# Laying out the weight loads of a DMA-bound decode kernel for the DMA engines

## The chip, the cores and the metric

The kernel runs on one core of one Trainium2 chip. The metric is the device time of one execution in microseconds (us). Most executions of one kernel agree within 0.1%, and all within 0.25%: the kernel before took between 2662.8 and 2669.3 us over all runs of this study, and its median was between 2663.6 and 2664.8 in every group of runs made together. So a difference of about 1 us between medians of two groups says little.

## The reference, cut to what matters

A decode step with batch 2 and one token goes twice through the same two blocks: attention over a long cache, and a small MLP.

```python
B, Sq, D = 2, 1, 576
H, Sk, Dh = 32, 16384, 128             # k_cache, v_cache: (B, H, Sk, Dh) in bf16, 268 MB each
q = (x @ wq) ...                       # wq (576, 4096)
p = softmax(q @ k_cache^T * Dh**-0.5);  o = p @ v_cache
x = x + o @ wo                         # wo (4096, 576)
...                                    # B block: hs = shift(gelu(LN(x) @ w1)) @ w2  (w2 576x576)
h2 = gelu(LN(x1) @ w3) @ w4            # w3 (576, 4608), w4 (4608, 576)
# x = x + A(x); x = x + B(x); x = x + A(x); x = x + B(x)
```

With one token the shifted input of `w2` is zero; the kernel still loads `w2` and multiplies it with zeros. All of K and V is read once per layer, which is over 1.06 GB in 508 loads of 2 MB (one of the 64 head-batch units is kept from the first layer to the second). The weights are some 40 MB of 1106 MB. 576 is 4 times 128 plus 64, so `wq` and `w3` have a last tile of only 64 rows.

## The kernel before

All loads go through one queue (the SP engine's) into a ring of 12 slots. A load is issued as soon as the readers of the slot that it overwrites are done.

```python
def kv(src, u, h):            # a half of K or V of a unit: 128 partitions x 16 KB
    ap = src[b, hh].rearrange("(t p j) d -> t p (j d)", t=2, p=128)[h]
    return lambda e, v: e.dma_start(v, ap)

def krows(w, k, c0, c1):      # wq, w3, w2: tile k, one row per partition
    if k < self.KT - 1:
        ap = w[k * 128:(k + 1) * 128, c0:c1]
        return lambda e, v: e.dma_start(v, ap)
    ap = w[k * 128:D, c0:c1]                                # the last 64 rows
    return lambda e, v: e.dma_start(v[self.p0:128, :], ap)  # p0 = 64: partitions 64 to 127

def jrows(w, j0, n):          # wo, w4: n blocks of 128 rows, rows of 1,152 bytes
    ap = w[j0 * 128:(j0 + n) * 128, :].rearrange("(j p) n -> p j n", p=128)
    return lambda e, v: e.dma_start(v.rearrange("p (j n) -> p j n", j=n), ap)

# the order of the loads of a layer (cut)
for i, u in enumerate(order):
    K(u, 0), K(u, 1)
    if l == 0 and i == 0: w2 in 5 loads (krows)
    if i >= 1: V(order[i - 1], 0), V(order[i - 1], 1)   # before every 16th: wo of 8 heads (jrows)
w3 in 5 loads (krows), w4 in 3 loads of 12 blocks (jrows); after layer 0: wq in 5 loads
```

Every 16 units `group_out` divides 16 columns by their sums, multiplies them with 8 heads of `wo` and adds to `x`. ... (cut: scores, half on PE and half on DVE; exponentials on ACT; the sum over V on PE.)

## Time and profile before

| what | number | where it is read |
|---|---|---|
| median time | 2663.6 us (3 runs), 2664.0 (4 runs with the changed kernel) | timings |
| DMA traffic | 1110.9 MB, mean 417 GB/s | page, DMA part |
| busy share | DVE 74%, PE 59%, ACT 41%, DMA about 99% | page, parts 1 and 3 |
| undisturbed slices | 425 to 427 GB/s | page, part 2 |

The rate of the 40 equal slices of the execution (66.6 us each), and the DMA queues (packets, MB, share of the time of 16 engines), from the page of the kernel before:

```profile
GB/s 393 426 426 427 424 419 426 426 426 408 426 426 426 426 407 426 426 426 425 357 401 421 426 426 422 426 427 425 426 392 426 426 427 426 407 426 426 427 426 300
q1 hardware_dynamic: 94072, 1106.16, 99.0%
q8 instruction: 270, 4.42, 0.7%
```

The kernel is bound by DMA: 1110.9 MB at 427 GB/s take 2602 us of 2663. The other 60 us are the dips: some at about 407 (a `wo` load is in that slice), the layer change (357, 401), and the end (392, 300). Queue q8 is the fetching of instructions.

What the `wo` load does to the queue, from the timeline of the SP engine (start, us until the next entry, what). It issues `wo` at 616.42, and then the next load of V takes 36 us to issue, and the one after it goes out at 657.1:

```profile
616.42 4.25 SPq L307 DMA_DIRECT2D ring<-in_A_wo_dram  x1
620.71 38.36 SPq L296 DMA_DIRECT2D ring<-in_A_v_cache_dram  x2
659.11 0.93 SPq L296 DMA_DIRECT2D ring<-in_A_k_cache_dram  x2
```

Waiting for the ring is not the reason: by the kernel's own semaphore counts the readers of these two slots were done at 613.5 and 623.3 us. So it was the queue that held the load up, behind `wo`.

The DMA issues of `wo` (count, KB each, us from issue to landing), and the layer change in the view by stretches (stretch in us; length; busy time and instructions of PE, PEld, DVE, ACT, POOL; clock; DMA share; GB/s):

```profile
ring<-in_A_wo_dram SPq DMA_DIRECT2D x8, 1152.0 KB, 48.7
1309.00:1361.00 52.00, 26.08 (x679) 24.69 (x680) 8.36 (x34) 4.71 (x12) 0.00 (x0) 0.50 1.02 334
```

Note the DMA share of 1.02 beside 334 GB/s: over these 52 us (w3, w4 and wq) the engines were occupied all the time, but moved a fifth less than they can. The loss is slow packets, not waiting. Around the two 64-row tiles of this stretch, one packet in twenty of `wq` took over 848 ns and of `w3` over 1,089 ns, where the median over the whole execution is 309 and 347.

The end, from the timeline: after the last piece of w4 lands, 60 matmuls, and then the output:

```profile
2658.41 1.76 PE L457 MATMUL misc<-gt,ring 128*128 128x2 bf16 x60 [2.75 <-DMA ring<-in_B_w_dram]
2661.87 0.28 SPq L405 DMA_DIRECT2D out_dram<-prod  x1
```

**Two groups of engines.** The trace also holds a record of every completion. A load over 128 partitions runs on 16 DMA engines and leaves 16 records. Sorted by time they fall into eight early and eight late ones. The records around the second `wo` load of the kernel before (us):

```
                 early eight        late eight
K unit 32, h 1   650.3 .. 652.5     659.6 .. 662.0
wo heads 8-15    653.1 .. 655.4     662.5 .. 664.9
V unit 31, h 0   663.3 .. 664.0     667.4 .. 669.8
V unit 31, h 1   668.2 .. 668.9     672.3 .. 674.7
```

The early eight are some 9 us ahead (I call this the lead). Behind the `wo` load they run dry, and lose about 5 us of it. The late eight go on: 2.9 us for `wo`, then 4.9 for the next load. Elsewhere a K or V load takes the early eight 4.89 us and the late eight 4.99 us on average: an interval of the late eight is 4.89 without an instruction fetch in it and about 5.08 with one, averaged over the eight. Of 497 such intervals 254 were of the long kind, and 263 fetches fell into the same stretch of time.

### The profile page before, as it was taken

Reading aid. Unit: us, or ns where it says so; the run is one execution under the profiler, and the core shown is the slowest. Engines: PE = TensorE matmul, PEld = TensorE weight load, DVE = VectorE, ACT = ScalarE, POOL = GpSimd, SP = SyncE. Lnnn points to the kernel's source line nnn. Section 1 sums busy time; section 2 is a strip of 40 time slices with the busy share of each in tenths; the row PEclk is TensorE's granted clock in tenths of the full one; section 3 lists DMA queues with packets and bytes.
Section 4 is the critical chain, followed back from the end, with each engine's and each line's share of the span. In section 5 each row is a group of like instructions: output and inputs, shape, how many; then the busy total and the mean of one; then the engine's idle time right before and its main releaser. Section 6 shows DMA issues by size and latency. Waiting matters only on the chain.

```text
span 2663.4 us, 74240 instructions
## 1 busy us (share of the span) xinstructions
PE 1558.8 (59%) x34587; PEld 1461.0 (55%) x34587; DVE 1979.6 (74%) x2649; ACT 1098.5 (41%) x1681; POOL 0.8 (0%) x10
## 2 busy tenths in 40 slices
PE   4665565555556555556467565665556556556654
PEld 4555555555555555555457555555555555555554
DVE  5877877777777777787559777777777777777773
ACT  3444344344334434434235344344334434434431
POOL 0000000000000000000000000000000000000000
PEclk8666666666666666666566666666666666666665
DMA  9999999999999999999999999999999999999998
GB/s 393 426 426 427 424 419 426 426 426 408 426 426 426 426 407 426 426 426 425 357 401 421 426 426 422 426 427 425 426 392 426 426 427 426 407 426 426 427 426 300
DMA packets 94380, 1110.90 MB, mean 417 GB/s; under 512 B 8756, under 2 KB 26744, under 8 KB 26744
## 3 DMA queue, kind: packets, MB, share of 16 engines
q1 hardware_dynamic: 94072, 1106.16, 99.0%
q8 instruction: 270, 4.42, 0.7%
q14 instruction: 38, 0.31, 0.0%
HBM read 1106.13 MB, written 0.00 MB: 415 GB/s over the span
## 4 chain that ended last, share of the span: by engine, by line
DMA 67%; PE 11%; DVE 8%; another core or an unknown queue 8%; ACT 4%; SPq 1%; issue 1%
DMA ring<-in_A_v_cache_dram 35%; DMA ring<-in_A_k_cache_dram 28%; DVE sd L572 5%; PE ops L617 5%; PE tps L539 4%; DMA ring<-in_B_w_dram 4%; ACT ktsb L543 3%; DVE prod L569 3%; PE sps L557 1%; PE misc L590 1%; DMA ring<-in_A_wq_dram 1%; ACT p L603 1%; SPq L301 0%; PE misc L457 0%
## 5 line engine op out<-in xcount | busy, mean ns | idle before, releaser
L572 DVE TENSOR_REDUCE sd<-prod 128x8 f32<-128x1024 bf16 x1024 | 1249.0, 1220 | 35.4
L543 ACT ACTIVATE ktsb<-tps 128x1024 bf16<-128x1024 bf16 x1024 | 992.7, 1028 | 514.6 <-PE tps L539 509.1
L539 PE MATMUL tps<-ident,ring 128*128 128x128 bf16 x8192 | 829.2, 268 | 336.8 <-DMA ring<-in_A_k_cache_dram 336.8
L569 DVE TENSOR_TENSOR prod<-ring,qb 128x1024 bf16<-128x1024 bf16 x1024 | 698.7, 682 | 256.0 <-DMA ring<-in_A_k_cache_dram 255.3
L539 PEld LDWEIGHTS tps<-ident,ring 128*128 128x128 bf16 x8192 | 673.4, 123 | 366.5 <-DMA ring<-in_A_k_cache_dram 358.6
L617 PE MATMUL ops<-p,ring 128*128 128x1 bf16 x16384 | 471.2, 165 | 564.8 <-DMA ring<-in_A_v_cache_dram 555.2
L617 PEld LDWEIGHTS ops<-p,ring 128*128 128x128 bf16 x16384 | 450.1, 102 | 585.8 <-DMA ring<-in_A_v_cache_dram 571.7
L526 ACT ACTIVATE qb<-misc 128x128 bf16<-128x128 f32 x128 | 35.5, 277 | 941.8 <-PE misc L524 941.8
L557 PE MATMUL sps<-qt,ktsb 128*128 128x1 bf16 x8192 | 349.9, 166 | 93.4 <-ACT ktsb L543 85.1
L557 PEld LDWEIGHTS sps<-qt,ktsb 128*128 128x128 bf16 x8192 | 313.0, 102 | 132.8 <-ACT ktsb L543 131.6
L592 DVE TENSOR_REDUCE bias<-misc 128x1 f32<-128x128 f32 x128 | 37.3, 291 | 260.6 <-PE misc L590 260.6
L590 PE MATMUL misc<-identS,m 128*128 128x128 f32 x256 | 95.5, 476 | 34.6 <-DVE m L584 34.6
L590 PEld LDWEIGHTS misc<-identS,m 128*128 128x128 f32 x256 | 69.7, 333 | 37.2 <-DVE m L584 37.1
L603 ACT ACTIVATE p<-sps,bias 128x64 bf16<-128x64 f32 x128 | 40.5, 317 | 23.8 <-DVE bias L592 23.8
L603 ACT ACTIVATE p<-sd,bias 128x64 bf16<-128x64 f32 x128 | 45.4, 354 | 0.0
L448 PE MATMUL sps<-xn,ring 128*128 128x2 bf16 (+1 forms) x680 | 20.6, 165 | 30.0 <-DMA ring<-in_A_wq_dram 15.6
L448 PEld LDWEIGHTS sps<-xn,ring 128*128 128x128 bf16 (+1 forms) x680 | 19.4, 104 | 31.2 <-DMA ring<-in_A_wq_dram 13.8
L524 PE MATMUL misc<-ident,qt 128*128 128x128 bf16 x128 | 34.3, 268 | 2.2 <-DVE xa L649 1.6
L580 DVE TENSOR_REDUCE m<-sps 128x1 f32<-128x64 f32 x128 | 27.4, 214 | 0.0
L603 ACT ACTIVATION_READ_ACCUMULATOR p<-sps,bias 128x1 f32 x128 | 27.1, 212 | 0.0
L582 DVE TENSOR_REDUCE m<-sd 128x1 f32<-128x64 f32 x128 | 26.6, 208 | 0.0
L603 ACT ACTIVATION_READ_ACCUMULATOR p<-sd,bias 128x1 f32 x128 | 26.5, 207 | 0.0
(63 smaller groups left out, 123.4 us busy)
## 6 DMA issues: line engine op xcount, KB each, us to landing
ring<-in_A_k_cache_dram SPq DMA_DIRECT2D x254, 2048.0 KB, 46.5
ring<-in_A_v_cache_dram SPq DMA_DIRECT2D x254, 2048.0 KB, 50.4
ring<-in_B_w_dram SPq DMA_DIRECT2D x6, 1728.0 KB, 35.5
ring<-in_A_wo_dram SPq DMA_DIRECT2D x8, 1152.0 KB, 48.7
ring<-in_B_w_dram SPq DMA_DIRECT2D x8, 1152.0 KB, 23.4
ring<-in_A_wq_dram SPq DMA_DIRECT2D x8, 1024.0 KB, 10.6
ring<-in_B_w_dram SPq DMA_DIRECT2D x2, 576.0 KB, 31.9
ring<-in_A_wq_dram SPq DMA_DIRECT2D x2, 512.0 KB, 16.6
```

What stands on the lines that cost most here:

```text
L448: ins = pe.matmul(out[:, m * self.B:(m + 1) * self.B], lhsT=w[lo:128, m * 128:(m + 1) * 128], rhs=self.xn[lo:128, k, :], start=(k == 0 and ...
L524: self.pe(lambda pe: pe.matmul(self.misc[:, 0:128], lhsT=bcast(self.qt[:, u:u + 1], 128), rhs=self.ident[:, :], start=True, stop=True), r= ...
L526: self.act(lambda a: a.activation(out=self.qb[q][:, :], in_=self.misc[:, 0:128], func=ACT.Copy), r=["P:misc"], w=[f"qb{q}"])
L539: ins = pe.transpose(self.tps[b][:, j * 128:(j + 1) * 128], kt[:, (j0 + j) * 128:(j0 + j + 1) * 128], self.ident[:, :])
L543: self.act(lambda a: a.activation(out=self.ktsb[k][:, :, :].rearrange("p a b -> p (a b)"), in_=self.tps[b][:, :], func=ACT.Copy), r=[f"P:t ...
L557: ins = pe.matmul(self.sps[sp][:, col:col + 1], lhsT=self.ktsb[k][:, j, :], rhs=self.qt[:, u:u + 1], start=True, stop=True)
L569: self.dve(lambda v: v.tensor_tensor(out=self.prod[d][:, :, :], in0=k3, in1=bcast_mid(self.qb[q][:, :], self.CH), op=ALU.mult), r=[res, f" ...
L572: self.dve(lambda v: v.tensor_reduce(out=self.sd[q][:, o:o + self.CH], in_=self.prod[d][:, :, :], axis=AX.X, op=ALU.add), r=[f"prod{d}"], ...
L590: self.pe(lambda pe: pe.matmul(self.misc[:, 128:256], lhsT=bcast(self.m[:, q:q + 1], 128), rhs=self.identS[:, :], start=True, stop=True), ...
L592: self.dve(lambda v: v.tensor_reduce(out=self.bias[:, q:q + 1], in_=self.misc[:, 128:256], axis=AX.X, op=ALU.max, negate=True), r=["P:misc ...
L603: self.act(lambda a, c0=c0, c1=c1, src=src, part=part: a.activation(out=self.p[q][:, c0:c1], in_=src, func=ACT.Exp, bias=self.bias[:, q:q ...
L617: ins = pe.matmul(self.ops[g][:, col:col + 1], lhsT=vt[:, j * 128:(j + 1) * 128], rhs=self.p[q][:, h * self.TB + j:h * self.TB + j + 1], s ...
```

## The change

Its intent is to give the DMA engines fewer and longer rows, to take `wo` out of the ring and off the SP queue, and to spread the last 64 rows of `wq` and `w3` over all partitions. The core of the diff:

```diff
-    GH = 8
+    GH = 2
+    FJ = 4
+    W4_PIECES = (3, 3, 2, 1)
+        self.wobuf = sb("wobuf", [128, self.GH, self.D], BF16)
 # last rows of wq and w3: two loads of 64 partitions, each with about half of the columns
-            ap = w[k * 128:D, c0:c1]
-            return lambda e, v: e.dma_start(v[self.p0:128, :], ap)
+            a0, a1 = w[k * 128:D, 0:cut], w[k * 128:D, n - cut:n]
+            return cut, [lambda e, v: e.dma_start(v[0:64, 0:cut], a0),
+                         lambda e, v: e.dma_start(v[64:128, 0:cut], a1)]
 # w4: four rows of 1,152 bytes per partition are one run of 4,608 bytes
+        def frows(a0, n):
+            ap = self.w4[a0 * 128 * self.FJ:(a0 + n) * 128 * self.FJ, :].rearrange(
+                "(a p j) n -> p a (j n)", p=128, j=self.FJ)
 # w2: one load over 96 partitions in runs of 6,912 bytes, at the third unit
-                if l == 0 and i == 0:
-                    for k in range(self.KT):
-                        ring.want(("w2", k), D, krows(self.w2, k, 0, D), aligned=(k == 0))
+                if l == 0 and i == 2:
+                    ap = self.w2.rearrange("(p r) n -> p (r n)", p=96)
+                    ring.want(("w2",), 6 * D, [lambda e, v: e.dma_start(v[0:96, :], ap)])
 # wo: 2 heads at a time into its own buffer, issued by ACT
-            self.ring.want(("wo", l, h0), self.GH * self.D, jrows(self.wo, h0, self.GH))
+    def load_wo(self, l, i):
+        h0 = self.group_base(l, i)
+        ap = self.wo[h0 * 128:(h0 + self.GH) * 128, :].rearrange("(j p) n -> p j n", p=128)
+        self.s.dma(lambda e: e.dma_start(self.wobuf[:, :, :], ap), w=["wobuf"], eng="scalar")
```

... (cut: w3's weights are read with a step of 4 columns to match w4's rows; the matmuls of the last tile use one weight tile for two column blocks, with the last 64 values of x once on the lower and once on the upper partitions and zeros elsewhere; group_out runs 32 times instead of 8.)

## The prediction

> **What bounds it now.** The page shows 16 DMA engines busy nearly throughout, 1110.9 MB moved, and 426-427 GB/s in undisturbed slices. At that rate the bytes alone need about 2600 us of 2663.4, so at most some 60 us are losable, and compute (DVE 74%, PE 59%) is not the limit. Slices with a `wo` load fall to about 407 GB/s, the layer change to 401 and 357, the last two to 392 and 300.
>
> **Where those 60 us are.** Each K/V load gives 16 completion records. Between disturbances eight engines take 4.89 us per load and eight take 4.98, and the gap between the two groups grows to 7-15 us. The slow eight are delayed by instruction fetches (queue q8, 270 packets of 16 KB, 1.07 us each against 0.61 for a K/V packet). The slow group finishes last and decides the time; this costs about 45 us, which the change does not touch.
>
> Around every `wo` load the fast group stops for about 5 us, because the SP queue then holds its next V load back 34-38 us (DMA timeline) behind 1,024 short rows. But the slow group goes straight on: its interval over the `wo` load is 2.9 us against 2.77 for the bytes. So the eight 407 GB/s dips look like 2-3 us each but cost the critical engines about 0.15 us each. **I therefore expect almost none of the visible `wo` dip to return as time.**
>
> The real losses on the slow group: the 64-partition last tiles of `wq` and `w3`. Their packets take 600-1,090 ns instead of 309 and 347, and neighbours slow too. Summed over intervals this is about 2 us at the start, 9 us at the layer change, 6 us at the end. `w4` in 1,152-byte rows takes 4.4-4.5 us per load against 4.14: about 1.5 us in all. After the last landing, 60 matmuls (1.76 us) run.
>
> **What the change does.**
> - `wo`, 32 loads of 288 KB on ACT: the same short rows, now interleaved with K/V. The Trainium skill ("DMA: Bandwidth & Descriptors", Issuing engines are not separate DMA queues) says they share the 16 engines; this trace has no second data queue to check it. 0 to +4 us, with group_out 32 times instead of 8 (about 2 us of PE/DVE each, not critical).
> - Last tiles over both halves: each DMA still reaches only 64 partitions. The skill's rule in the same page (Rules for kernel authors) says transfers to disjoint halves serialize on the same engines. Contention is spread over both halves rather than removed; I expect about half of 17 us back: -8.
> - `w4` in 4.6 KB rows: -1.5. Last piece 20 matmuls instead of 60: -1.1.
> - `w2` in one load: about -0.3. Strided weights for w3: hidden under loads.
>
> **Prediction:** 2654 us (0.4% less), 8 in 10 between 2641 and 2664. Faster by over 2%: 0.02; within 2%: 0.95; slower by over 2%: 0.03.
>
> **Signs.** Right: the 407 GB/s dips vanish from the slices and yet under 15 us come back; the gap between fast and slow completions grows past 15 us because nothing resets it; K/V issue no longer stalls 34-38 us at `wo`; w4 packets at full bytes per ns; the last w4 wait is followed by 20 matmuls. If the split works, no packets of w3/wq stay at 600-1,090 ns; if it doesn't, their packets remain at twice the time per byte.
>
> **What would make it wrong.** `wo` on a second queue costing switching time on every engine, as instruction fetches do (each delays its engine about 1.45 us): then slower by 10 us or more. ACT blocked while issuing, delaying the K copies. The fast group's stalls mattering after all (its lead may feed slot releases): then 20 us or more come back. The split removing all contention: about 2643.

## More of the kernel before

(Six of the eight `wo` loads show in slices inside the layers, four of them as dips to 392 to 408; the other two fall into the slices of the layer change and of the end.)

The V load after each of the eight `wo` loads took 31.0 to 42.3 us to issue (the prediction has 34 to 38), each time with its slot free before the issue began; no other load of K or V took more than 12.1.

## The result, and the profile after

The changed kernel took 2665.37 us (median of 4 runs, 2664.3 to 2666.8), the kernel before 2663.97 us (4 runs). The ratio is 1.0005, with a 95% interval of 0.9988 to 1.0023: the same. (Ratios are the mean time of one kernel's fast runs over that of the other's in the same rounds, so not quite the ratio of the quoted medians.) The predicted 2654 us, with a range of 2641 to 2664, is missed on the high side.

The same lines of the page after:

```profile
GB/s 383 425 426 426 424 425 425 426 425 426 425 425 425 426 425 425 425 425 425 358 386 411 425 425 425 425 425 425 426 426 425 426 424 425 427 424 425 425 425 270
q1 hardware_dynamic: 78648, 1096.86, 97.9%
q10 hardware_dynamic: 8704, 9.44, 1.0%
q8 instruction: 271, 4.44, 0.7%
```

All dips of 407 inside the layers are gone; q10 is ACT's new queue with `wo`. But the other slices now read 425 where they read 426, and the slices of the layer change and of the end look no better (although the view by stretches, below, has 365 GB/s at the layer change). The SP timeline has no stall at the same place any more, and the issues of `wo` land in 15 us:

```profile
610.89 9.21 SPq L311 DMA_DIRECT2D ring<-in_A_k_cache_dram  x2
620.15 8.55 SPq L311 DMA_DIRECT2D ring<-in_A_v_cache_dram  x2
628.74 11.62 SPq L311 DMA_DIRECT2D ring<-in_A_k_cache_dram  x2
...
wobuf<-in_A_wo_dram ACTq DMA_DIRECT2D x32, 288.0 KB, 15.3
```

The layer change in the view by stretches (as above: 334 GB/s before):

```profile
1314.00:1366.00 52.00, 29.76 (x699) 27.99 (x697) 13.63 (x43) 9.46 (x17) 0.00 (x0) 0.53 0.99 365
```

The end has its shorter tail, 20 matmuls instead of 60:

```profile
2658.56 0.69 PE L519 MATMUL misc<-gt,ring 128*128 128x2 bf16 x20 [0.17 <-DMA ring<-in_B_w_dram]
2660.96 0.28 SPq L433 DMA_DIRECT2D out_dram<-prod  x1
```

So three things that the change aimed at happened, and the time did not move. To see where it went, I cut each profiled execution at the same loads, by the mean time of the eight late completion records, in us:

| run | start, to V of unit 1 | layer 1 | layer change | layer 2 | end | lead before w3, layer 1 and 2 |
|---|---|---|---|---|---|---|
| before | 68.8 | 1239.3 | 56.8 | 1259.5 | 39.1 | 5 and 3 |
| before, two copies in effect (b3, b4) | 67.9, 67.7 | 1239.5, 1239.3 | 58.2, 57.9 | 1260.2, 1259.5 | 40.5, 39.7 | 5 and 2 to 3 |
| after | 70.8 | 1241.6 | 52.9 | 1263.2 | 34.1 | 25 and 28 |

The layer change runs from the last V load of layer 1 to the first unit's K in layer 2; the end runs from the last V load to the end of the execution. The two copies show that these stage times repeat within about 1.5 us. The changed kernel gains 4 to 5 us at the layer change and 5 to 6 at the end, and gives it back: 2 to 3 us at the start, 2.3 in layer 1 and 3.7 in layer 2. And the lead of the early engines grows to 28 us, since nothing stops them any more.

### The profile page after: what moved, and what is told of

The parts are those of the page before. It is cut to its first block, busy times and chain, and to the rows that moved or that the text cites. A ratio compares the mean times of both kernels' runs of the same rounds, so it can differ in the third digit from the quotient of the medians.

```text
span 2662.5 us, 74385 instructions
## 1 busy us (share of the span) xinstructions
PE 1570.4 (59%) x34580; PEld 1473.5 (55%) x34580; DVE 1994.0 (75%) x2753; ACT 1097.5 (41%) x1681; POOL 0.9 (0%) x11
## 4 chain that ended last, share of the span: by engine, by line
DMA 74%; DVE 24%; PE 1%; issue 1%; SPq 0%; ACT 0%; DVEq 0%
DMA ring<-in_A_k_cache_dram 69%; DVE sd L639 15%; DVE prod L636 9%; DMA ring<-in_A_v_cache_dram 4%; DMA ring<-in_A_wq_dram 1%; DMA ring<-in_B_w_dram 1%; PE sps L480 0%; PE misc L657 0%; PE ops L684 0%; SPq L319 0%; SPq L321 0%; PE misc L446 0%; PE misc L448 0%; PE misc L519 0%; DVE bias L659 0%
## 5 line engine op out<-in xcount | busy, mean ns | idle before, releaser
L639 DVE TENSOR_REDUCE sd<-prod 128x8 f32<-128x1024 bf16 x1024 | 1249.4, 1220 | 35.4
L657 PE MATMUL misc<-identS,m 128*128 128x128 f32 x256 | 95.4, 476 | 30.8 <-DVE m L651 30.8
L519 PE MATMUL misc<-otn,wobuf 128*128 128x2 bf16 x320 | 13.7, 168 | 93.3 <-DVE otn L703 93.3
L519 PEld LDWEIGHTS misc<-otn,wobuf 128*128 128x128 bf16 x320 | 11.0, 105 | 96.3 <-DVE otn L703 96.3
L591 PE MATMUL misc<-ident,qt 128*128 128x128 bf16 x128 | 34.9, 272 | 11.8 <-DVE xa L713 7.8
L480 PE MATMUL sps<-xn,ring 128*128 128x2 bf16 x544 | 18.4, 169 | 17.0 <-DMA ring<-in_A_wq_dram 10.5
L480 PEld LDWEIGHTS sps<-xn,ring 128*128 128x128 bf16 x544 | 17.4, 111 | 17.9 <-DMA ring<-in_A_wq_dram 8.9
## 6 DMA issues: line engine op xcount, KB each, us to landing
ring<-in_A_k_cache_dram SPq DMA_DIRECT2D x254, 2048.0 KB, 47.4
wobuf<-in_A_wo_dram ACTq DMA_DIRECT2D x32, 288.0 KB, 15.3
```

The lines of the kernel that those rows point to most:

```text
L480: ins = pe.matmul(out[:, m * B:(m + 1) * B], lhsT=pick(w, g, j), rhs=self.xn[:, k, :], start=(k == 0 and m == 0), stop=False, skip_group_c ...
L591: self.pe(lambda pe: pe.matmul(self.misc[:, 0:128], lhsT=bcast(self.qt[:, u:u + 1], 128), rhs=self.ident[:, :], start=True, stop=True), r= ...
L639: self.dve(lambda v: v.tensor_reduce(out=self.sd[q][:, o:o + self.CH], in_=self.prod[d][:, :, :], axis=AX.X, op=ALU.add), r=[f"prod{d}"], ...
L657: self.pe(lambda pe: pe.matmul(self.misc[:, 128:256], lhsT=bcast(self.m[:, q:q + 1], 128), rhs=self.identS[:, :], start=True, stop=True), ...
```

## The experiments

Two theories ran through them. Theory S is the prediction's: the late eight engines set the time, and every term is to be summed on them. Its rivals say that the dips of the whole core are what counts, or compute.

### One part undone (a1 to a4, 5 rounds each)

Each is the changed kernel with one part as it was before.

```diff
 # a1_wo_back
-    GH = 2
+    GH = 8
-                if i % n == 1 and c == 6:
-                    self.load_wo(l, i)
+            self.ring.want(("wo", l, h0), self.GH * self.D, jrows(self.wo, h0, self.GH))
 # a2_w2_back
-                if l == 0 and i == 2: ...   # one load over 96 partitions
+                if l == 0 and i == 0: ...   # five loads as before
 # a3_tiles_back
-            return cut, [lambda e, v: e.dma_start(v[0:64, 0:cut], a0),
-                         lambda e, v: e.dma_start(v[64:128, 0:cut], a1)]
+            return n, [lambda e, v: e.dma_start(v[self.p0:128, :], ap)]
 # a4_w4_back
-                ring.want(("w4", l, c), n * self.FJ * D, frows(a0, n), aligned=False)
+                ring.want(("w4", l, c), n * self.FJ * D, jrows(self.w4, a0 * self.FJ, n * self.FJ), aligned=False)
```

> The changed kernel with only its wo part undone (eight 1,152 KB loads on the SP queue, in the ring, group_out 8 times). Theory S (the eight DMA engines that finish last set the time): on them a 288 KB wo load cost 0.84 us in the changed kernel against 2.95/4 = 0.74 before, and about 1 us more per layer end, so 4 to 7 us come back: 2658 to 2661. The 407 GB/s dips return to the slices all the same. Rival D (the dips of the whole core are the loss): the eight dips of 2 to 3 us come back, so it is slower than the changed kernel by 15 us or more: 2680.

> The changed kernel with only its w2 part undone (five loads of 1,152-byte rows, first unit). Theory S: the 96-partition load took 4.7 us on the late engines, the five loads 1.8 us, so 2 to 3 us come back: 2662.5 to 2663.5. Rival (longer rows are what counts, as the prediction had it): 0.3 us slower than the changed kernel.

> The changed kernel with only the split of the last wq and w3 rows undone (one load to partitions 64 to 127 again). Theory S with the prediction's share: 6 to 9 us slower, 2672 to 2674, with packets of 600 us-thousandths and more back at the layer change. Rival (the gain at the layer change and at the end is w4's and the longer lead of the early engines'): within 2 us of the changed kernel.

(The "600 us-thousandths" of the last text are nanoseconds.)

> The changed kernel with only the w4 rows undone (1,152-byte rows, unit-step weights for w3; the pieces 3,3,2,1 stay). Theory S: 0.2 to 0.3 us per load, 1 to 2 us slower in all, 2666.5 to 2667.5. Rival (the 4.6 KB rows carry most of what the layer change and the end gained): 5 us slower or more.

The kernel before had a median of 2664.83 us beside these four (9 runs).

| run | median, us | start | layer 1 | change | layer 2 | end | lead |
|---|---|---|---|---|---|---|---|
| after (its own group of runs) | 2665.37 | 70.8 | 1241.6 | 52.9 | 1263.2 | 34.1 | 25, 28 |
| a1, wo undone | 2662.64 | 69.8 | 1239.3 | 55.0 | 1259.7 | 37.1 | 7, 6 |
| a2, w2 undone | 2664.53 | 68.6 | 1241.5 | 53.3 | 1263.1 | 35.9 | 25, 28 |
| a3, tiles undone | 2666.75 | 70.4 | 1241.9 | 54.0 | 1263.2 | 35.0 | 25, 28 |
| a4, w4 undone | 2664.97 | 70.3 | 1241.5 | 51.4 | 1262.9 | 34.9 | 25, 27 |

- The rival of the dips falls: in a1 the `wo` dips come back (four of its slices inside the layers read 404 to 408 again), and the kernel is 2.7 us faster, not 15 slower. That is less than the 4 to 7 us expected. The two layers give back 5.8 us, but with the lead gone the layer change and the end take 5 us more.
- a2 gives back its 2.2 us at the start; the median shows 0.8, less than the 2 to 3 expected. Longer rows did not help w2. Its 96-partition packets took 442 ns (median) for 6,912 bytes, 15.7 bytes per ns, where a K/V packet has 26.7.
- a3 is the surprise: undoing the split, on which 8 us of the prediction rested, costs 1.4 us, hardly more than the medians of two groups of runs differ by. The rival (the gain at the change and at the end comes from the longer lead, not from the split) fits.
- a4: the 4.6 KB rows of w4 are worth nothing that can be measured (0.4 us the other way, where 1 to 2 us were expected).

The layers of a1 (1239.3, as before) put the price of `wo` in the two layers of the changed kernel at 5.8 us. About half of that comes from its 32 small loads; where the rest lies is shown by g2 below. In the long stretch of layer 1 that holds only K, V and `wo`, the late eight needed 0.83 us per load of 288 KB, in that of layer 2 0.93; before it was 2.95 us per 1,152 KB, which is 0.74 per 288. Over 16 loads in each layer that is 1.4 and 3.0 us, between 4 and 5 in all.

### Only wo (d1, 5 rounds)

The kernel before with only the `wo` part of the change: 32 loads on ACT; tiles, w4 and w2 undone as in a2 to a4, and w4 in three pieces of 12 blocks again.

> The kernel before with only the wo part of the change (32 loads of 288 KB on ACT); tiles, w4 and w2 as before. Theory L (the loss at the layer change and at the end is contention between the early and the late eight engines when both are within a few us of the 64-row tiles; with wo off the SP queue the lead stays at about 25 us and they no longer meet): the two layers cost 6.5 us more, but the layer change and the end 3 and 4 us less, so 2663 to 2666 in spite of the unsplit tiles, lead at the last V load 24 to 28 us. Rival (the gain there is the split's and w4's): about 6.5 us slower than before, 2670 to 2672, the layer change at 56 to 58 us as before.

Measured: 2664.51 us against 2664.84 for the kernel before (ratio 0.9999, 0.9986 to 1.0013). Stages: start 68.7, layers 1241.8 and 1263.3, change 53.4, end 35.4. So with the old, unsplit tiles and the old w4, the layer change and the end are already within 0.5 and 1.3 us of the changed kernel's. Moving `wo` alone costs 6.3 us in the layers and returns 7.1 us at the change and at the end. That is the place of the missing time: what the split was to gain had been gained by the lead, and the lead was paid for in the layers. In the view by stretches d1's layer change reads:

```profile
1313.00:1365.00 52.00, 28.10 (x702) 26.49 (x699) 13.29 (x40) 9.84 (x17) 0.00 (x0) 0.54 0.91 326
```

The rate, 326 GB/s, is lower than before (334), and yet this stage is 3.4 us shorter than in the kernel before. The rate of the whole core is no measure of the time here either.

### The queue or the small loads (b1, 5 rounds; b2, 3 rounds)

```diff
 # b1_wo_sp2: the same 32 loads, issued by SP
-        self.s.dma(lambda e: e.dma_start(self.wobuf[:, :, :], ap), w=["wobuf"], eng="scalar")
+        self.s.dma(lambda e: e.dma_start(self.wobuf[:, :, :], ap), w=["wobuf"])
 # b2_wo_act1: 64 loads of one head on ACT
-    GH = 2
+    GH = 1
```

> The changed kernel with its 32 wo loads of 288 KB into the same buffer, but issued from SP instead of ACT: only the queue differs. If the second queue costs (switching between queues on each engine): back to the level of the kernel with wo undone, 2658 to 2660. If the cost is in the 32 small loads themselves: as the changed kernel, 2664 to 2666.

> The changed kernel with wo by 1 head: 64 loads of 144 KB on ACT, same bytes and rows. If each load on the second queue has a fixed cost of about 0.15 to 0.2 us on the late engines: 5 to 6 us slower than the changed kernel, about 2671. If the cost goes with the rows or the bytes: unchanged within 1.5 us.

b1 took 2663.49 us and b2 2667.35, with 2664.43 for the kernel before. The layers of b1 are those of the changed kernel (1241.6 and 1263.3), so the second queue is not what costs. But the same loads issued by SP land late, behind all that is queued there:

```profile
wobuf<-in_A_wo_dram SPq DMA_DIRECT2D x32, 288.0 KB, 47.4
```

In b2 the layers grow by 1.4 and 0.9 us (1243.0 and 1264.1) with 16 more loads each: a small cost per load, under 0.1 us here. Both medians lie between the two outcomes that I had foreseen, so neither run decides by its time. b1's is 1.9 us below the changed kernel's, but they come from two groups of runs, so I don't build on that.

### Two attempts that changed nothing (b3, b4, 3 rounds each)

b3 was to add 16,384 no-ops on PE, b4 to put four V loads on eight DMA engines by describing the source as 8 groups of 16 rows. (The rule of the Trainium skill that b4, e1 and g1 name is in "DMA: Bandwidth & Descriptors", Why a DMA increments its semaphore by 16 and not by 1.)

```diff
 # b3_nops (in turn)                          # b4_eight (in kv)
+                for _ in range(2):           +            if src is self.V and h == 1 and u % 32 == 8:
+                    pe.nop()                 +                ap = ap.rearrange("(e q) n -> e q n", e=8)
```

> The kernel before with two no-ops on PE before each key transpose: 16,384 instructions more, about 64 instruction fetches of 16 KB more; PE is 59% busy. Theory S: a fetch delays its engine by 1.5 us and eight engines share them, so 64 * 1.5 / 8 = 12 us slower, 2676 (10 to 14). Rival (only the bytes count, on all 16 engines alike): 1 MB at 427 GB/s, 2.5 us. Rival (compute decides): as PE time grows, no relation to the fetches of the late engines; the interval of the late eight stays 4.98.

> The kernel before with 4 of its 508 K/V loads (V, second half, units 8 and 40, both layers) described to the DMA with their source rows as 8 groups of 16, so that by the Trainium skill's rule for the number of engines they run on 8 engines only. Theory S, if those are the early eight: the late eight lose four loads, 4 * 4.98 = 20 us faster, 2644; if they are the late eight: about 20 us slower, 2684. Each of these loads then shows 8 completion records instead of 16. Rival (no group decides): 0 to 10 us slower. If 16 records remain, the description had no effect and the time is that of before.

Neither did what it was built for. b3's page has the instruction count of the kernel before, and b4's four loads still left 16 completion records. The first line of b3's page, and its fetch queue (271 fetches, where the kernel before has 270, so the no-ops are not in the program at all):

```profile
span 2666.2 us, 74240 instructions
...
q8 instruction: 271, 4.44, 0.7%
```

Both took 2664.99 us. They say nothing about the theory, but serve as copies of the kernel before in the stage table.

### Do instruction fetches on the late engines set the time? (e2, e1, 3 rounds each)

e2 repeats the fetch experiment with real instructions, e1 the experiment with eight engines by cutting four V loads into loads of 8 partitions:

```diff
 # e2_twice, on the kernel before (in score)
                 col = c * self.CH + j
+                pe.matmul(self.sps[sp][:, col:col + 1], lhsT=self.ktsb[k][:, j, :], rhs=self.qt[:, u:u + 1],
+                          start=True, stop=True)
 # e1_eight, on a1 (in kv)
+            if src is self.V and h == 1 and u % 32 == 8:
+                return [lambda e, v, p=p: e.dma_start(v[p:p + 29:4, :], ap[p:p + 29:4, :])
+                        for q in range(4) for p in range(q * 32, q * 32 + 4)]
```

> The kernel before with every score matmul done twice (same result): 16,384 PE instructions more, about 64 fetches of 16 KB more, PE about 350 us busier of 2,663. Theory S: 64 * 1.52 / 8 = 12 us slower (10 to 14), the mean interval of the late eight 5.01 to 5.02 instead of 4.99, that of the early eight unchanged at 4.90. Rival (bytes on all 16 engines alike): 2.5 us. If compute decided: the interval of the early eight would grow too.

> The changed kernel with wo undone (a1) and with 4 of the 508 K/V loads cut into 16 loads of 8 partitions (4 apart), which by the Trainium skill's rule run on engines 0 to 7 only; 8 completion records each. Theory S, if engines 0 to 7 are the early eight: the late eight lose 4 * 4.99 us, about 20 us faster than a1: 2643. If they are the late eight: about 20 us slower, 2682. Rival (no group of engines decides): 0 to 10 us slower than a1.

e2 took 2676.44 us, 11.6 us more than the kernel before (2664.84; ratio 1.0044, 1.0031 to 1.0058). From its page, the first lines and the fetch queue:

```profile
span 2674.7 us, 90624 instructions
...
PE 1781.5 (67%) x42779; PEld 1708.8 (64%) x42779; DVE 1980.0 (74%) x2649; ACT 1108.3 (41%) x1681; POOL 0.8 (0%) x10
...
q8 instruction: 335, 5.49, 0.8%
```

There are 65 more fetches, about 1 MB, which at 427 GB/s would be 2.5 us. The interval of the late eight went from 4.990 to 5.011 us per K/V load; that of the early eight stayed at 4.90. This is what theory S had said in numbers: a fetch holds up one of eight engines by about 1.5 us, and these eight decide. Compute is ruled out as the cause, since it would hold up both groups. This also shows where most of the loss inside the layers lies: at the same rate (an estimate from 11.6 us for 65 fetches) the 270 fetches that the kernel has anyway cost some 48 us. No run here tried fewer instructions.

e1 took 2718.23 us, 55.6 more than a1: neither of the two outcomes foreseen (20 us faster or slower), so what follows is a reading after the fact. Each small load left eight records of data, and one that comes at the issue. That is as the Trainium skill says ("DMA: Bandwidth & Descriptors", Why a DMA increments its semaphore by 16 and not by 1: the number of engines divides the number of partitions, and the sequencer writes the rest at once). Their times continue those of six early and two late engines. So my assumption that the lowest eight engines are one of the groups was wrong. The two late ones needed 18.6 us for 16 rows, against 4.99 us for their 8 rows of an ordinary load. Four times that difference is 54 us, which is the time the kernel lost. The other engines had slack, and it didn't help. These loads were not clean, though: 16 rows at the 0.61 us of a K/V row would be 9.8 us, not 18.6.

### What the last 64 rows cost (c1, c2, g2, h1, 5 rounds each)

If 64-partition loads are the loss, no split into two of them can cure it. c2 cuts each of the 64 rows in two and lays the halves on neighbouring partitions, one load over 128 partitions; x's last 64 values are laid on even and on odd partitions by a matmul with a 0/1 matrix. c1 is the changed kernel with `wo` and w2 undone; c2 is c1 with the new layout.

```diff
 # c2_interleave against c1_keep_good
-    FJ = 4
-    W4_PIECES = (3, 3, 2, 1)
+    FJ = 3
+    W4_PIECES = (4, 4, 3, 1)
-            a0, a1 = w[k * 128:D, 0:cut], w[k * 128:D, n - cut:n]
-            return cut, [lambda e, v: e.dma_start(v[0:64, 0:cut], a0),
-                         lambda e, v: e.dma_start(v[64:128, 0:cut], a1)]
+            ap = w[k * 128:D, :].rearrange("r (h n) -> (r h) n", h=2)
+            return cut, [lambda e, v: e.dma_start(v, ap)]
...
+        for h in range(2):          # spl[64 + r, h, r, h] = 1: row r goes to partition 2r + h
+            self.dve(lambda v, h=h: v.tensor_copy(out=self.spl[64:128, h, :, h], in_=self.ident[64:128, 64:128]), ...)
 # g2_after_inter: the same layout on the changed kernel (wo on ACT, w2 in one load)
 # h1_fj3: c1 with FJ = 3 and W4_PIECES = (4, 4, 3, 1) alone
```

> The changed kernel with wo and w2 undone, and the last 64 rows of wq and w3 laid out in one load over 128 partitions (each row cut in two halves on neighbouring partitions; w4 in rows of 3.4 KB, pieces 4,4,3,1). If the 64-partition loads are the loss at the layer change and at the end (contention at the partitions' ports): their packets take 155 to 180 ns, both stages shorten to 48 to 50 and 27 to 29 us, and it beats all so far: 2651 to 2655. Rival (contention comes from early and late engines being at different loads whatever their shape): 2660 to 2662, as with wo undone alone.

> The changed kernel with only the layout of the last rows of wq and w3 altered: one load over 128 partitions (and w4 with it in rows of 3.4 KB). wo on ACT and w2 stay. If the 64-partition loads cost even when the early engines are 25 us ahead: layer change 48 to 50 us instead of 53, end 29 instead of 32, so 5 to 8 us faster than the changed kernel, about 2658. If the lead alone had removed that loss: within 2 us of the changed kernel, 2664 to 2666.

> The changed kernel with wo and w2 undone and nothing else: c2 without the layout over 128 partitions. From a1 and a2: 2659.5 to 2661.5. The difference to c2 (2645.7) is then what the layout of the last rows is worth where the lead is small: 14 to 16 us. If c1 is below 2655, the parts undone interact and the layout is worth less.

> c1 with w4 in rows of 3.4 KB and pieces 4, 4, 3, 1 as in c2, the last rows of wq and w3 still split over two loads of 64 partitions. If c2's 15 us come from the layout of the last rows: as c1, 2659 to 2662, packets of the split loads still at 262 and about 300 ns. If they come from w4's new pieces: 2645 to 2650.

| run | median, us | before, same group | ratio (95%) | start | layer 1 | change | layer 2 | end |
|---|---|---|---|---|---|---|---|---|
| c1 | 2660.67 | 2664.61 | 0.9984 (0.9971 to 0.9997) | 68.2 | 1239.3 | 55.2 | 1259.6 | 36.5 |
| h1 | 2657.87 | 2664.78 | 0.9974 (0.9960 to 0.9988) | 67.9 | 1239.2 | 54.2 | 1259.5 | 35.2 |
| c2 | 2645.70 | 2664.84 | 0.9928 (0.9915 to 0.9940) | 66.6 | 1239.3 | 47.1 | 1260.3 | 30.8 |
| g2 | 2651.51 | 2664.61 | 0.9949 (0.9936 to 0.9963) | 69.3 | 1239.9 | 47.5 | 1261.5 | 30.8 |

The new layout is worth 15.0 us against c1, of which h1 has 2.8 with w4's other pieces (and without the columns that the split loads twice), so about 12 us for the layout (all from medians of different groups). On the changed kernel it is worth 13.9 us, whatever the lead. c2 beats both kernels, by 0.7%. The packets of the last rows, from the trace (median ns of one packet, and bytes per ns):

```
                       wq rows              w3 rows
split (after)          4096 B: 262, 15.6    5120 B: 345.5, 14.8
128 partitions (c2)    4096 B: 159, 25.8    4608 B: 178, 25.9
```

The Trainium skill ("SBUF — State Buffer", Door 1: The DMA port swizzle) says that partitions 0 to 63 reach only 8 of the 16 ports through which the DMA writes, and partitions 64 to 127 only the other 8. The time per byte, 1.65 and 1.75 times that of the loads over 128 partitions, points the same way, though it is not the full factor of two. The rates of the slices, first c2, then g2, and then the layer change of c2 in the view by stretches (to be set beside that of the kernel before, which had 334 GB/s):

```profile
GB/s 406 426 426 427 425 425 426 426 426 408 427 427 425 426 392 427 426 426 426 416 422 410 426 426 418 427 426 426 426 408 426 426 425 427 404 426 427 425 426 341
GB/s 392 425 426 426 425 425 425 426 425 425 425 425 425 425 426 425 425 424 426 372 417 411 425 426 424 426 425 425 425 425 426 425 425 425 426 426 425 426 425 298
1307.00:1359.00 52.00, 30.70 (x754) 28.42 (x754) 19.38 (x48) 11.92 (x20) 0.00 (x0) 0.57 1.02 424
```

c2 keeps all its `wo` dips to 392 to 408 and is the fastest of all; g2 has none of them and is 5.8 us slower (about 2 of that is w2 in one load). The DMA share of the stretch is 1.02 as before, at 424 instead of 334 GB/s: the same occupation, full packets.

g2 also corrects the account of `wo`. The changed kernel's layers were 2.3 and 3.7 us longer than before; in g2, with the same `wo`, they are 0.6 and 2.0 longer. The difference, 1.7 us per layer, sits in the last two V loads: there the early engines, 25 us ahead, are already at the 64-row tiles, and disturb the late ones at V. In g2 these four half loads take 19.9 us, as four intervals of 4.99 should, in the changed kernel 21.6. So the small loads of `wo` themselves cost some 3 us in the two layers (0.6 and 2.0 in g2; 4 to 5 by the intervals above).

### Which engines are early (g1, one look)

```diff
 # g1_probe, on c2
+    FEW = {8: 114, 20: 115, 32: 124, 44: 119}      # unit: partitions of the first of two loads
+            if n:
+                return [lambda e, v: e.dma_start(v[0:n, :], ap[0:n, :]),
+                        lambda e, v: e.dma_start(v[n:128, :], ap[n:128, :])]
```

> c2 with the second half of V of four units cut in two loads of 114, 115, 124 and 119 partitions and the rest; by the Trainium skill's rule they run on the lowest 6, 5, 4 and 7 engines. The completion records of each tell how many, and their times against the load before whether these engines are early or late ones. From e1: of engines 0 to 7 six are early. No claim on the time.

The loads left 6, 5, 4 and 7 records and one at the issue, so the rule for the number of engines holds. But the load of 114 partitions took its six engines over 20 us, where 19 rows at 0.61 us would be 11.6, and the whole took 2866 us. The disturbance hides which engines were early. Moving bytes from the late to the early engines, which by theory S would be worth up to 20 us more, I could therefore not try: no load at hand runs on early engines alone, and short sets of engines disturb all others. That stays open.

## Why the prediction was wrong

| term of the prediction | predicted, us | measured, us |
|---|---|---|
| split of the last rows | -8 (half of 17) | -1.4 (a3) with the long lead; with the short lead at most -3.9 together with w4 and the tail (c1), where -10.6 was predicted for the three; a layout that avoids the 64-row loads gains 14 to 15 more (g2, c2 against c1, w4's pieces included) |
| w4 in long rows | -1.5 | none (a4: 0.4 the other way) |
| shorter tail | -1.1 | -1.0 (last landing to the end: 5.0 before, 4.0 after) |
| w2 in one load | -0.3 | +2.2 at the start (a2), 0.8 in the median |
| wo in 32 loads on ACT | 0 to +4 | +3 to +5 for the loads; -7 at the change and the end (d1), +3.4 at the last V loads, with the lead |

- **Right:** that the visible `wo` dips are not time. They vanished, nothing came back, and c2 is the fastest with the dips in place. That the late eight engines set the time was confirmed with e2 (12 us said, 11.6 measured); e1 missed both of its stated outcomes and fits only as read afterwards. The size of the loss at the 64-row tiles was about right (17 said, 14 to 15 recovered by c2 and g2, of which about 12 are the layout alone). The signs came as said: the lead grew past 15 us, the SP stalls went, 20 matmuls follow the last wait.
- **The step that failed:** "Contention is spread over both halves rather than removed; I expect about half of 17 us back: -8." Each half is still a load on 64 partitions, and its packets ran at 15 bytes per ns where 26 are possible, close to the prediction's own sign for failure ("their packets remain at twice the time per byte"). Where the lead was short, as in the kernel before, from which the 17 us were summed, the split, w4's rows and the shorter tail together gave 3.9 us (c1 against the kernel before, ratio 0.9984, 0.9971 to 0.9997), of which the tail is 1; where the lead was long, the split gave 1.4. I had cited the skill's rule that two transfers to disjoint halves serialize ("DMA: Bandwidth & Descriptors", Rules for kernel authors), and then discounted it by half with no measurement behind the half.
- **A second failure:** w2. I counted longer rows as a gain, but the load on 96 partitions ran as slowly as those on 64: 15.7 bytes per ns. Whether an uneven use of the ports is the reason was not tested.
- **What was not foreseen:** that the lead and the tiles interact. With `wo` off the queue (d1) the layer change and the end shrank by 7 us without any new layout, which is why the total of after over d1 shows nearly nothing of the split. d1 shows that this happens with the `wo` part alone; it moves the SP stalls and the lead together. Why a lead of 25 us makes unsplit 64-row loads cheaper at w3, w4 and wq I have only argued: the early engines are then at other loads when the late ones come to these tiles. No run shows the mechanism.

So the unchanged time is a sum of small terms of both signs. The tail (-1) and the earlier end and layer change by the lead (-7) are set against the disturbance at the last V loads (+3.4), small `wo` loads (+3) and w2 (+2.2); the split and w4's rows were small. The terms add up to about +1, and +1.4 was measured, both within what two groups of runs differ by.

## What to carry to other kernels

In a DMA-bound kernel take the completion records of each load apart by engine before costing a change: the group that finishes last sets the time, and a dip in the rate of the whole core can be idleness of engines that have slack. Give every load 128 partitions; a tile of 64 rows is better cut so that each row lies on two partitions than sent to half of them, or to both halves one after the other. When a change touches several loads, undo one part at a time, and do one part alone too, since parts can hide each other.

## What the Trainium skill lacked or had wrong

- "DMA: Bandwidth & Descriptors" has nothing on instruction fetches holding up some of the DMA engines, nor has "Runtime: NRT & Kernel Launch", where fetches are described. Here eight of the sixteen engines needed 4.99 us per 2 MB load and the others 4.89, and 65 fetches more (1 MB) cost 11.6 us.
- "DMA: Bandwidth & Descriptors" (Latency and other measured facts) says that engines 7 and 15 are usually slower; it guesses at a cause in DMAs issued by GpSimd, of which this kernel has none. Here eight engines were late (4.99 us per load against 4.89), and by e1 two of them are among engines 0 to 7 and so six among 8 to 15.
- The same page (Rules for kernel authors) says not to split a transfer over disjoint partition halves, and that was right: the split packets ran at 15 bytes per ns against 26. It says to use one transfer over 128 partitions instead; it lacks how a tile of 64 rows becomes one, and the price in a kernel: 12 to 14 us over four such tiles here, gone when each row was cut over two partitions.
- "SBUF — State Buffer" (Door 1) has the port rule for 64 partitions. It gives no rate for 96 partitions (here 15.7 bytes per ns), and none for the neighbours: loads over 128 partitions beside a 64-row tile were slowed too (the stretch with w3, w4 and wq moved 334 GB/s, and 424 without such tiles).
- The first of these pages (Issuing engines are not separate DMA queues) agrees: `wo` from SP or from ACT cost the layers the same (1241.6 us both). What that section lacks is that the queue makes a difference to the time to landing (15.3 us on ACT, 47.4 on SP), and that a load of 1,024 short rows held up the issue of the next load of its queue for 31 to 42 us.
- No page says that no-ops on PE do not reach the chip as built here: 16,384 of them left the count at 74240 instructions and the fetches at 271.
